# Batches three and four of an attention and mixer kernel: a head pair's scores in one piece of TensorE work, with two PSUM banks lent by the first channel product, its weighted sums in one piece, and hand-set places for both

## The chip, the cores and the metric

One core of a Trainium2 chip runs the whole program in one launch. The metric is device time in microseconds (us), the median of several executions. TensorE (PE) multiplies matrices into PSUM, which has eight banks of 512 fp32 columns on 128 partitions; VectorE (DVE) and ScalarE (ACT) read PSUM; GpSimd (POOL) works on SBUF alone; SyncE (SP) issues nearly all DMAs, in order. Each engine runs its own queue in order and waits on semaphores for the others.

## The reference

Four batches, 8 heads, 768 positions, head dimension 64. Attention over a local window plus block summaries, then a mixer over tokens and one over channels:

```python
mask_l = np.abs(pos[:, None] - pos[None, :]) < 16
k_sum = k.reshape(B, H, nb, 32, D).max(axis=3); v_sum = v.reshape(B, H, nb, 32, D).mean(axis=3)
scores_l = np.where(mask_l, scale * q @ k.T, -1e9)
scores_s = scale * q @ k_sum.T + np.log(32)
a = softmax(concatenate([scores_l, scores_s]));  attn = a @ concatenate([v, v_sum])
x = attn, heads side by side                           # (4, 768, 512)
h = np.maximum(x.T @ w_tok1, 0) @ w_tok2;  u = x + h.T  # tokens: 768 -> 256 -> 768
out = u + np.maximum(u @ w_ch1, 0) @ w_ch2             # channels: 512 -> 1536 -> 512
```

## The kernel before, in words

The program is written as a list of pieces of work (`add`, L91), each with an engine, an estimated duration, what it reads and writes and a rank. `Plan` (L77) lays the list out in time with those estimates: whenever an engine is free it takes the ready piece of lowest rank, then the oldest. The order that comes out is fixed for each engine before the kernel runs. On the chip an engine that meets a piece whose inputs are not there waits, with all that is queued behind it. Buffers and PSUM banks are rings with a tag: a ring of n gives its next user the buffer of the user n places before, once all of that user's work is done (`_link`, L114).

While the channel products of batch b run, the attention and the token mixer of batch b+1 are put between them. The loop over b (L1622) has 24 slots: twelve steps f with 512 of the 768 positions (half 0), then twelve with 256 (half 1). In a slot `ch1` (L926) adds the first channel product of the next step: 12 matmuls into one bank (`hp`, ring "mm", 2 banks), a relu on ACT (L947), its rounding rest on DVE (L952). `ch2` (L962) adds the second product of this step: 12 matmuls into the banks acc0 to acc3 in half 0, acc0 and acc1 in half 1. Both have rank `R_W`, below that of attention, so they fill PE whenever nothing else is ready.

PSUM: two banks have the tag "att", two "mm", four "acc". In half 0 attention has "att" alone (`BANKS[0]`, L263); in half 1 it also has acc2 and acc3.

Attention goes by pairs of heads, four pairs a batch. In the third and fourth batch (`FAR = 2`) a pair takes these steps (`att_step`, L685, in the order `LATER`, L672):

- `scores(p, g)` for each half g of the positions (L438): 24 PE instructions into two banks `sc`, one for each head; then six times `lowest` on DVE (L478: adds the mask, writes the negated scores to the SBUF tile `e`, and gives the row's extreme) and six times the exponential on ACT (L488). PSUM is free after the last `lowest`.
- `turn_blocks(p, g)` (L575): a transpose of `e` on DVE (L583), one DMA to DRAM (`away`, L587), four DMAs back (`eT`, L602).
- `weighted(p)` (L612): for each head 24 PE instructions into a bank `av` (L630), the reciprocals (L643, L647), a scaling out of PSUM on DVE (L650). Then `turn_x` (L711) sends the result to DRAM, and `load_v` fetches the next values.

The tiles `e`, `eT` and `xb` of `turn_x` share the ring "e" of three. `tok2` (L852) is the second token product for a pair and half: 6 PE instructions into a bank `up` (L874), an addition of the residual `xT` on DVE (L891), and a split into two parts (L901, L907). For half 1 it stands in slots 2 to 5 of the batch's own loop (`u1s`, L1632), with `fetch_x` (L733) one slot ahead, four DMAs to `xT`. The attention steps of the next batch are spread evenly over slots `a0` to `a1` (L1630, L1679). In the loop of b = 2, `weight_away` (L1102) writes one 512 KB block of weights to DRAM in each of slots 12 to 23. A Strassen-like scheme (`last_mix`, L1176) does the last batch's channel products after the loops.

Of the kernel before, what the change touches and what calls it, by code (L numbers as in the profile page):

```python
# [24 lines left out]
P = 128  # L25
# [177 lines left out]
def tile_attention_mixer(  # L203
# [234 lines left out]
    def scores(p, g, behind=()):  # L438

        kt, qt = k_t[p], q_t[p]  # L440
        tiles = []
        e = e_t[p, g] = sbuf([P, 2, HS], "e", f"e_{p}_{g}", 3)
        if p >= FAR * NP:

            add(
                "pool", 0.2,
                lambda: nc.gpsimd.memset(
                    e.t.rearrange("p j (t c) -> p (j t) c", c=P)[:, :, NC:], 0.0
                ),
                writes=[(e, "ends")], rank=R_LATER,  # L450
            )
        for j in range(2):
            n = 2 * p + j
            if g == 0:
                den_t[n] = sbuf([P, 2, TT], "den", f"den_{n}", 5)
            tiles.append(att_bank(f"sc_{n}_{g}"))

        def products():
            for i in range(TT // 2):
                for c in range(2):  # L460
                    t = 2 * (TT // 2 * g + i) + c
                    for j in range(2):
                        rows = slice(j * D, (j + 1) * D)
                        nc.tensor.matmul(  # L464
                            tiles[j].t[c * QT : (c + 1) * QT, i * NC : (i + 1) * NC],
                            lhsT=qt.t[rows, t * QT : (t + 1) * QT], rhs=kt.t[rows, t, :],
                            start=True, stop=True,
                        )
# [6 lines left out]
        def lowest(n, j, i):  # L475
# [3 lines left out]
                out=e.t[:, j, i * P : i * P + NC],  # L479
                in0=tiles[j].t[:, i * NC : (i + 1) * NC],  # L480
# [4 lines left out]
        def power(n, j, i):  # L485
            T = TT // 2 * g + i
            ei = e.t[:, j, i * P : i * P + NC]
# [8 lines left out]
        for j, i in parts:  # L496
                n = 2 * p + j
                den, T = den_t[n], TT // 2 * g + i
# [1266 lines left out]
```

## Time and profile before

| | us |
|---|---|
| median of 3 runs (549.94 to 551.34) | 551.19 |
| the profiled execution | 551.51 |
| its span, first to last instruction | 549.4 |

The profile gives, for each engine, every instruction with its start and duration, what ended the idle time ahead of it, and a chain of waits followed back from the last instruction. The duration of a matmul in the timeline includes a modelled end that overlaps the next one, so the cost of a piece of PE work is read from its start to the start of the next piece. PEld is the weight load that belongs to each matmul and overlaps others. The loop of b = 1, which carries the third batch's attention, runs from 191 to 323 us; the loop of b = 2, with the fourth's, from 323 to 457.

### The profile page before, as it was taken

The page shows a single profiled execution, that of the slowest core. Times are in us where ns is not written, and L with a number is a line of the kernel's source. Part 1 is how long each engine was busy: PE and PEld are TensorE (multiplying, and loading weights), DVE is VectorE, ACT ScalarE, POOL GpSimd, SP SyncE. Part 2 cuts the span into 40 slices and gives each one's busy share as a digit, 9 for nine tenths or more (in the row PEclk, how much of TensorE's full clock was granted, in tenths as well). Part 3 has the DMA queues.
Part 4 walks back from the last instruction along what each step waited for, and adds up shares of the span by engine and source line. Part 5 has one row for each costly group of instructions (what it writes and reads, how often), then busy time and mean ns, then how long its engine had stood idle before and what let it go on. Part 6 is the DMA issues. An engine that isn't in the chain of part 4 may idle for free.

```text
span 549.4 us, 12914 instructions
## 1 busy us (share of the span) xinstructions
PE 538.9 (98%) x4649; PEld 477.7 (87%) x4649; DVE 341.4 (62%) x954; ACT 268.9 (49%) x771; POOL 268.8 (49%) x348
## 2 busy tenths in 40 slices
PE   7999999999999999999999999999999999999997
PEld 4789888878999978788899988878799999999997
DVE  4996778667556654565653536544443584787886
ACT  4897888755574242223342334322334443566652
POOL 2656688713036110398996220069979602445111
PEclk9999999999999999999999999999999999999999
DMA  8963798664658357869796427668787654543521
GB/s 323 397 202 116 220 269 241 205 189 143 213 150 249 64 143 169 240 195 274 189 279 165 68 56 187 162 177 235 193 247 241 184 225 144 181 135 118 189 98 57
DMA packets 148127, 103.46 MB, mean 188 GB/s; under 512 B 101216, under 2 KB 126048, under 8 KB 148064
## 3 DMA queue, kind: packets, MB, share of 16 engines
q1 hardware_dynamic: 147920, 102.55, 63.2%
q8 instruction: 36, 0.59, 0.4%
q14 instruction: 27, 0.22, 0.1%
q10 hardware_dynamic: 144, 0.10, 0.1%
HBM read 70.96 MB, written 29.88 MB: 184 GB/s over the span
## 4 chain that ended last, share of the span: by engine, by line
PE 88%; DMA 6%; SPq 1%; issue 1%; ACT 1%; POOL 1%; DVE 0%; DVEq 0%; POOLq 0%; ACTq 0%
PE acc L978 26%; PE hp L935 25%; PE up L874 6%; PE t1q L833 5%; PE av L630 4%; PE pb L1213 3%; PE qb L1213 3%; PE sc L464 3%; PE qc L1213 2%; PE pa L1213 2%; PE pc L1213 2%; PE qa L1213 2%; PE t1p L785 2%; DMA w<-in_w_tok 2%; DMA vw<-in_vw 2%; DMA q<-in_q 1%
## 5 line engine op out<-in xcount | busy, mean ns | idle before, releaser
L978 PE MATMUL acc<-h,w 128*128 128x512 f32 (+1 forms) x864 | 162.2, 337 | 0.0
L935 PE MATMUL hp<-u,w 128*128 128x512 f32 (+1 forms) x864 | 161.1, 336 | 0.0
L935 PEld LDWEIGHTS hp<-u,w 128*128 128x128 f32 x864 | 132.9, 188 | 18.0 <-issue 1.3
L978 PEld LDWEIGHTS acc<-h,w 128*128 128x128 f32 x864 | 131.8, 188 | 19.0 <-ACT h L947 1.7
L947 ACT ACTIVATE h<-hp 128x512 fp32r<-128x512 f32 (+1 forms) x72 | 35.3, 490 | 121.2 <-PE hp L935 118.8
L488 ACT ACTIVATE e<-e,den 128x120 f32<-128x120 f32 x192 | 69.9, 385 | 49.0 <-DVE den L478 43.1
L952 DVE SCALAR_TENSOR_TENSOR h<-hp,h 128x512 fp32r<-128x512 f32 (+1 forms) x72 | 39.9, 554 | 70.6 <-ACT h L947 70.1
L1055 POOL TENSOR_TENSOR s<-s,w 128x256 f32<-128x256 f32 x84 | 62.2, 745 | 5.2
L478 DVE CUSTOM_DVE_ANT_0 e<-sc,mask_sb 128x120 f32<-128x120 f32 x192 | 41.5, 277 | 11.1 <-PE sc L464 7.9
L1017 POOL TENSOR_TENSOR ot<-ot,u 128x512 f32<-128x512 f32 (+1 forms) x24 | 23.7, 1013 | 41.4 <-issue 14.0
L1584 POOL TENSOR_TENSOR w<-wb,w 128x256 fp32r<-128x256 f32 x48 | 34.6, 742 | 11.5 <-ACT w L1578 11.2
L819 POOL TENSOR_TENSOR xs<-x,xs 128x512 fp32r<-128x512 f32 x18 | 23.5, 1308 | 32.5 <-ACT xs L814 32.5
L874 PE MATMUL up<-wt,t 128*128 128x512 f32 (+2 forms) x192 | 38.0, 340 | 0.6 <-DVE den L478 0.6
L874 PEld LDWEIGHTS up<-wt,t 128*128 128x128 f32 x192 | 30.7, 189 | 3.8 <-issue 1.0
L420 DVE TENSOR_REDUCE vs<-vb 96x8 f32<-96x256 f32 (+1 forms) x40 | 18.2, 460 | 18.0 <-DMA vb<-in_vb 18.0
L833 PE MATMUL t1q<-xs,ws 128*128 128x256 f32 x216 | 28.5, 283 | 0.0
L464 PEld LDWEIGHTS sc<-k,q 64*64 64x64 f32 x768 | 20.2, 132 | 9.4 <-issue 6.3
L464 PE MATMUL sc<-k,q 64*64 64x120 f32 x768 | 27.2, 271 | 0.9 <-DVE k L1057 0.9
L630 PEld LDWEIGHTS av<-v,eT 120*64 120x64 f32 x768 | 23.9, 138 | 4.6 <-issue 3.5
L351 DVE TENSOR_REDUCE ks<-k 128x24 f32<-128x768 f32 x16 | 15.1, 947 | 20.0 <-DMA k<-in_kw 20.0
L630 PE MATMUL av<-v,eT 120*64 120x64 f32 (+1 forms) x768 | 26.3, 224 | 0.9 <-DMA eT<-away 0.9
L833 PEld LDWEIGHTS t1q<-xs,ws 128*128 128x128 f32 x216 | 26.9, 190 | 0.2
(131 smaller groups left out, 849.6 us busy)
## 6 DMA issues: line engine op xcount, KB each, us to landing
w<-in_w_ch SPq DMA_DIRECT2D x48, 256.0 KB, 3.9
k<-in_kw SPq DMA_DIRECT2D x16, 720.0 KB, 6.7
v<-in_vw SPq DMA_DIRECT2D x24, 288.0 KB, 3.7
q<-in_q SPq DMA_DIRECT2D x16, 384.0 KB
away<-e SPq DMA_DIRECT2D x16, 384.0 KB, 3.1
eT<-away SPq DMA_DIRECT2D x64, 96.0 KB, 2.9
sums<-s SPq DMA_DIRECT2D x24, 256.0 KB, 2.9
w2d<-w SPq DMA_DIRECT2D x12, 512.0 KB, 4.5
```

Of the source, the lines that this page charges most:

```text
L464: nc.tensor.matmul(tiles[j].t[c * QT : (c + 1) * QT, i * NC : (i + 1) * NC], lhsT=qt.t[rows, t * QT : (t + 1) * QT], rhs=kt.t[rows, t, :], ...
L478: nc.vector.tensor_tensor_reduce(out=e.t[:, j, i * P : i * P + NC], in0=tiles[j].t[:, i * NC : (i + 1) * NC], in1=mask_sb[:, mv, :], op0=A ...
L488: nc.scalar.activation(ei, ei, AF.Exp, bias=den_t[n].t[:, 1, T : T + 1], scale=-1.0, accum_out=den_t[n].t[:, 0, T : T + 1] if p >= NP else ...
L630: nc.tensor.matmul(pv[cs, T], lhsT=eT(T % (TT // 2), c), rhs=v.t[:NC, 2 * T + c], start=True, stop=True,)
L833: nc.tensor.matmul(pt.t[:, 2 * P * k : 2 * P * (k + 1)], lhsT=ws[:, wp, T, ks], rhs=xs[:, xp, T], start=(c == 0 and k == 0 and T == 0 and ...
L874: nc.tensor.matmul(pt.t[:, :nt], lhsT=t1.t[:, part, ks], rhs=wt2[w].t[:, k, h0 : h0 + nt], start=(far and k == 0 and i == 0), stop=(k == D ...
L935: nc.tensor.matmul(pt.t[:, :nt], lhsT=w1_t[f].t[:, w, c], rhs=us[c].t[:, part], start=(i == 0), stop=(i == len(ops) - 1),)
L947: lambda: nc.scalar.activation(h.t[:, 0], pt.t[:, :nt], AF.Relu),
L952: lambda: nc.vector.scalar_tensor_tensor(out=h.t[:, 1], in0=pt.t[:, :nt], scalar=0.0, in1=h.t[:, 0].bitcast(F32), op0=ALU.max, op1=ALU.sub ...
L978: nc.tensor.matmul(slot.t[:, c0 : c0 + nt], lhsT=w2_t[f].t[:, w, o * P : (o + 1) * P], rhs=h.t[:, part], start=(f == 0 and w == 0 and part ...
L1055: nc.gpsimd.tensor_tensor(out=out_, in0=left, in1=right, op=op)
L1213: nc.tensor.matmul(bank_.t[:, cs], lhsT=w(i), rhs=x(j)[:, cs], start=first and n == 0, stop=True, skip_group_check=True,)
```

## The change

For the third and fourth batch `scores` takes both halves of a pair at once: 48 PE instructions as one piece into four banks. In half 0 the banks of the first half are taken from the ring "mm", those of the second from "att"; in half 1 all four from the attention ring. `weighted` hands PE both heads' products as one piece. The even spread gives way to a table, `PLACES`: scores of a batch's pairs (with their two `turn_blocks`) in slots -1 (the last slot of the loop before), 2, 6 and 11, weighted sums in slots 0, 6, 11, 17 (third batch) and 2, 6, 11, 14 (fourth). In half 1 `tok2` takes "mm" banks for some pairs (`NEAR`) and stands in slots 2, 2, 3, 3 and 0, 1, 2, 2. Five of the twelve `weight_away` go to the end of the loop of b = 1, the rest to slots 17 to 23 of b = 2. Instructions on data, their shapes and their number stay the same.

```diff
-    def scores(p, g, behind=()):
+    def scores(p, gs, behind=()):
...
+        tiles, wide = {}, len(gs) > 1
+        for g in gs:
+            e = e_t[p, g] = sbuf([P, 2, HS], "e", f"e_{p}_{g}", 3)
...
+            for j in range(2):
+                n = 2 * p + j
+                if g == 0:
+                    den_t[n] = sbuf([P, 2, TT], "den", f"den_{n}", 5)
+                near = wide and g == 0 and state["phase"] == 0
+                tiles[g, j] = (mm_bank if near else att_bank)(f"sc_{n}_{g}")
 
         def products():
-            for i in range(TT // 2):
...
+            for g in gs:
+                for i in range(TT // 2):
+                    for c in range(2):
+                        t = 2 * (TT // 2 * g + i) + c
+                        for j in range(2):
...
         add(
-            "pe", 0.95, products, reads=[(qt, 0), (kt, 0), (kt, 1)],
-            writes=[(t, 0) for t in tiles], rank=R_H, behind=behind,
+            "pe", 1.55 if wide else 0.95, products, reads=[(qt, 0), (kt, 0), (kt, 1)],
+            writes=[(t, 0) for t in tiles.values()], rank=R_H, behind=behind,
         )
...
-        for j, i in parts:
+        for g in gs:
+            for j, i in parts:
...
@@ weighted
-            add(
-                "pe", 0.8, products, reads=eT_t[n, 0][1] + eT_t[n, 1][1] + [(v, 0), (v, 1)],
-                writes=[(pt, 0)], rank=R_H,
-            )
+            reads = eT_t[n, 0][1] + eT_t[n, 1][1] + [(v, 0), (v, 1)]
+            whole += [(products, reads, pt)]
+            if b < FAR:
+                add("pe", 0.8, products, reads=reads, writes=[(pt, 0)], rank=R_H)
+            elif j:
+                runs, reads, banks = zip(*whole)
+                add(
+                    "pe", 1.6, lambda: [run() for run in runs], reads=sum(reads, []),
+                    writes=[(pt, 0) for pt in banks], rank=R_H,
+                )
...
@@ att_step
-        LATER += [("e", hp, 0), ("e", hp, 1)] + [("s", hp + 1, 0)] * more
-        LATER += [("a", hp, 0)] + [("s", hp + 1, 1)] * more
+    PAIR = [("s", None), ("e", 0), ("e", 1), ("a", 0)]
...
-        kind, hp, g = (LATER if b >= FAR else ORDER if b else FIRST)[s]
+        if b >= FAR:
+            hp, (kind, g) = s // 4, PAIR[s % 4]
+        else:
+            kind, hp, g = (ORDER if b else FIRST)[s]
...
-            scores(p, g, behind)
+            scores(p, (0, 1) if g is None else (g,), behind)
...
-            if g == 0 and p not in (NP - 1, 2 * NP - 1):
+            if g != 1 and p not in (NP - 1, 2 * NP - 1):
                 key_blocks(p + 1)
-            if b and g == 1 and p + 2 < B * NP and (b > 1 or hp < NP - 2):
+            if b and g != 0 and p + 2 < B * NP and (b > 1 or hp < NP - 2):
                 load_k(p + 2)
                 load_q(p + 2)
@@ tok2
+    NEAR = (0, 1, 2), (0, 2)
...
-        pt = tok_bank(f"up_{b}_{half}_{p}")
+        name = f"up_{b}_{half}_{p}"
+        pt = mm_bank(name) if b and half and p in NEAR[b > 1] else tok_bank(name)
@@ the loop
+    PLACES = {2: {}, 3: {}}
+    for b, ss, aa in ((2, (-1, 2, 6, 11), (0, 6, 11, 17)), (3, (-1, 2, 6, 11), (2, 6, 11, 14))):
+        for hp in range(NP):
+            PLACES[b].setdefault(ss[hp], []).extend(range(4 * hp, 4 * hp + 3))
+            PLACES[b].setdefault(aa[hp], []).append(4 * hp + 3)
...
-            a0, a1 = 0, 29
             t1s = (18, 20)
-            u1s = (2, 3, 4, 5)
+            u1s = ((2, 2, 3, 3), (0, 1, 2, 2))[b - 1]
...
-                if b >= XFAR and u1s[p] == slot + 1:
+                if b >= XFAR and slot == max(u1s[p] - 1, 0):
                     fetch_x(b, 1, p)
...
+            else:
+                steps = PLACES[b + 1].get(slot, ())
...
-            if b == B - 2 and slot >= NF:
+            if b == B - 3 and slot >= 2 * NF - 5:
+                weight_away(slot - 2 * NF + 5)
+            if b == B - 2 and slot >= NF + 5:
                 weight_away(slot - NF)
...
+            if slot == 2 * NF - 1 and b + 2 < B:
+                for s in PLACES[b + 2].get(-1, ()):
+                    att_step(b + 2, s, here)
             ch2(b, half, f)
```

## Rows read from the trace of the kernel before

**Rows 1.** The page's first two parts: busy time of each engine, its share of the span and its instructions; then the clock granted to TensorE in 40 equal slices, in tenths of full speed (9 is 90% or more).

```profile
PE 538.9 (98%) x4649; PEld 477.7 (87%) x4649; DVE 341.4 (62%) x954; ACT 268.9 (49%) x771; POOL 268.8 (49%) x348
PEclk9999999999999999999999999999999999999999
```

**Rows 2.** The timeline of PE at the start of the loop of b = 1: start us, duration us, line, output and inputs, shape, count of instructions, and in brackets idle time ahead and what ended it.

```profile
194.53 3.01 PE L935 MATMUL hp<-u,w 128*128 128x512 f32 x12
197.47 0.85 PE L464 MATMUL sc<-k,q 64*64 64x120 f32 x24
...
201.84 0.95 PE L874 MATMUL up<-wt,t 128*128 128x256 f32 x6 [0.58 <-DVE den L478]
202.62 2.89 PE L935 MATMUL hp<-u,w 128*128 128x512 f32 x12
205.44 0.85 PE L464 MATMUL sc<-k,q 64*64 64x120 f32 x24
206.22 3.02 PE L978 MATMUL acc<-h,w 128*128 128x512 f32 x12
209.08 2.88 PE L935 MATMUL hp<-u,w 128*128 128x512 f32 x12
211.80 0.88 PE L874 MATMUL up<-wt,t 128*128 128x256 f32 x6
```

**Rows 3.** The timeline of PE in the first batch, where both halves of a pair's scores stand side by side, and the weight loads (PEld) of that piece and of a single one.

```profile
12.90 1.46 PE L464 MATMUL sc<-k,q 64*64 64x120 f32 x48 [0.85 <-DVE k L1057]
14.29 0.55 PE L560 MATMUL et<-identf,e 128*120 128x128 f32 x3
...
12.87 1.26 PEld L464 LDWEIGHTS sc<-k,q 64*64 64x64 f32 x48 [1.07 <-PE et L560]
...
205.44 0.62 PEld L464 LDWEIGHTS sc<-k,q 64*64 64x64 f32 x24 [0.35 <-issue]
206.22 0.76 PEld L978 LDWEIGHTS acc<-h,w 128*128 128x128 f32 x4 [0.16 <-ACT h L947]
```

**Rows 4.** The timeline of PE at weighted sums of the third and fourth batch: 48 instructions are both heads.

```profile
242.57 1.62 PE L630 MATMUL av<-v,eT 120*64 120x64 f32 x48
244.12 2.11 PE L935 MATMUL hp<-u,w 128*128 128x512 f32 x8
...
346.31 1.62 PE L630 MATMUL av<-v,eT 120*64 120x64 f32 x48
...
367.87 0.57 PE L630 MATMUL av<-v,eT 120*64 120x64 f32 x12
369.36 1.27 PE L630 MATMUL av<-v,eT 120*64 120x64 f32 x36 [0.92 <-DMA eT<-away]
```

**Rows 5.** The chain of waits in order of time: start us, us, what; the weighted sums of the third batch's first pair.

```profile
218.14 1.74 PE av L630 x48
```

**Rows 6.** The timeline of ACT, DVE and PE: the evacuation of the `hp` product that began at 202.62; score chunks on DVE (the first and the last of six that ran without a wait, then two that waited, one with the end of its six); and the channel piece that followed the scores of that last one.

```profile
205.61 0.60 ACT L947 ACTIVATE h<-hp 128x512 fp32r<-128x512 f32 x1 [1.42 <-PE hp L935]
207.92 0.65 DVE L952 SCALAR_TENSOR_TENSOR h<-hp,h 128x512 fp32r<-128x512 f32 x1
...
200.60 0.27 DVE L478 CUSTOM_DVE_ANT_0 e<-sc,mask_sb 128x120 f32<-128x120 f32 x1
201.61 0.28 DVE L478 CUSTOM_DVE_ANT_0 e<-sc,mask_sb 128x120 f32<-128x120 f32 x1
...
210.29 0.28 DVE L478 CUSTOM_DVE_ANT_0 e<-sc,mask_sb 128x120 f32<-128x120 f32 x1 [0.69 <-DMA away<-e]
...
364.79 0.28 DVE L478 CUSTOM_DVE_ANT_0 e<-sc,mask_sb 128x120 f32<-128x120 f32 x1 [1.76 <-DMA away<-e]
366.01 0.09 DVE L478 DVE_READ_ACCUMULATOR2_ANT den<- 128x1 f32 x1
...
359.48 3.02 PE L978 MATMUL acc<-h,w 128*128 128x512 f32 x12
```

**Rows 7.** The timeline of SP's DMA queue: fetches of `eT`, the load of `k` ahead of a write `away` that landed late (issued at 357.88), and the fetch that waited for it.

```profile
236.31 2.67 SPq L602 DMA_DIRECT2D eT<-away  x4
...
338.59 5.47 SPq L602 DMA_DIRECT2D eT<-away  x8
...
355.10 0.59 SPq L291 DMA_DIRECT2D k<-in_kw  x1
...
364.67 2.67 SPq L602 DMA_DIRECT2D eT<-away  x4
```

**Rows 8.** DMA issues, from the page's last part: count, KB each, median us to landing.

```profile
eT<-away SPq DMA_DIRECT2D x64, 96.0 KB, 2.9
```

**Rows 9.** Channel pieces of half 1 with nothing between them, and two that have other pieces nearby (timeline of PE); then the stretches that `weight_away` enters and leaves: length, busy us of PE, PEld, DVE, ACT and POOL with counts, granted clock, DMA share, GB/s.

```profile
315.57 1.58 PE L935 MATMUL hp<-u,w 128*128 128x256 f32 x12
316.98 1.58 PE L978 MATMUL acc<-h,w 128*128 128x256 f32 x12
...
290.29 1.52 PE L935 MATMUL hp<-u,w 128*128 128x256 f32 x12
291.65 1.52 PE L978 MATMUL acc<-h,w 128*128 128x256 f32 x12
...
302.00:322.00 20.00, 20.00 (x162) 19.52 (x161) 9.00 (x15) 6.06 (x13) 3.35 (x5) 1.00 0.30 49
402.00:438.00 36.00, 36.00 (x317) 35.21 (x316) 14.99 (x29) 12.75 (x28) 28.66 (x28) 1.00 0.75 219
```

More of the change, by code (lines that the diff above doesn't have):

```diff
@@ new lines, in scores @@
+        tiles, wide = {}, len(gs) > 1
+        for g in gs:
+            e = e_t[p, g] = sbuf([P, 2, HS], "e", f"e_{p}_{g}", 3)
+            if p >= FAR * NP:
+                add(
+                    "pool", 0.2,
+                    lambda e=e: nc.gpsimd.memset(
+                        e.t.rearrange("p j (t c) -> p (j t) c", c=P)[:, :, NC:], 0.0
+                    ),
+                    writes=[(e, "ends")], rank=R_LATER,
+                )
[5 more added lines that the diff above has]
+                tiles[g, j] = (mm_bank if near else att_bank)(f"sc_{n}_{g}")
@@ new lines, in products @@
+        def products():
+            for g in gs:
[3 more added lines that the diff above has]
+                        for j in range(2):
+                            rows = slice(j * D, (j + 1) * D)
+                            nc.tensor.matmul(
+                                tiles[g, j].t[c * QT : (c + 1) * QT, i * NC : (i + 1) * NC],
+                                lhsT=qt.t[rows, t * QT : (t + 1) * QT], rhs=kt.t[rows, t, :],
+                                start=True, stop=True,
+                            )
@@ L478, in lowest @@
             nc.vector.tensor_tensor_reduce(
-                out=e.t[:, j, i * P : i * P + NC],
-                in0=tiles[j].t[:, i * NC : (i + 1) * NC],
+                out=e_t[p, g].t[:, j, i * P : i * P + NC],
+                in0=tiles[g, j].t[:, i * NC : (i + 1) * NC],
                 in1=mask_sb[:, mv, :], op0=ALU.add, op1=ALU.min,
@@ L617, in weighted @@
         x_t[b, hp] = x2, hp % 2
+        whole, rest = [], []
         for j in range(2):
@@ L654, in scaled @@
                 )
-            add(
-                "pe", 0.8, products, reads=eT_t[n, 0][1] + eT_t[n, 1][1] + [(v, 0), (v, 1)],
-                writes=[(pt, 0)], rank=R_H,
-            )
+            reads = eT_t[n, 0][1] + eT_t[n, 1][1] + [(v, 0), (v, 1)]
[4 more added lines that the diff above has]
+                runs, reads, banks = zip(*whole)
+                add(
+                    "pe", 1.6, lambda: [run() for run in runs], reads=sum(reads, []),
+                    writes=[(pt, 0) for pt in banks], rank=R_H,
+                )
+            rest += [(inverse, scaled, pt, den, rec, j)]
+        for inverse, scaled, pt, den, rec, j in rest:
+            n = 2 * p + j
             add(
@@ L1678, in tile_attention_mixer @@
                         vb_step(b + 2, 2 * (slot - m0) + c)
-            want = -(-(start[slot + 1] - a0) * STEPS // (a1 - a0))
-            steps = range(done, max(done, min(STEPS, want)))
-            done = steps.stop
+            if b + 1 < FAR:
+                want = -(-(start[slot + 1] - a0) * STEPS // (a1 - a0))
+                steps = range(done, max(done, min(STEPS, want)))
+                done = steps.stop
+            else:
+                steps = PLACES[b + 1].get(slot, ())
             for s in steps:
```

42 lines of the change are left out of this document (10 added, 32 removed).

## The prediction, as it was put on record

> **What bounds the kernel now.** First the page's busy shares and its 40 slices: PE is busy 98% of the span, at the upper of its two clock levels (2.4 GHz) from end to end, with no other engine over 62% [rows 1]. The reader should see that the clock has nothing to give and that a change pays only in what PE does or waits for. The change adds and removes no instruction, so I look for two things: what PE loses where a small piece of work stands between large ones, and where it stands idle. I take both from PE's timeline in the two loops that the change touches, 191 to 457 us, since PE is booked solid there: the idle time that is shown in it is 0.58 us ahead of an `up` [rows 2] and 0.92 us inside one pair of weighted sums [rows 4].
>
> **The price of a small piece.** From start to start, a 512-column channel piece with like pieces on both sides takes 211.80 - 209.08 = 2.72 us. With scores ahead of it, it takes 209.08 - 206.22 = 2.86; with scores ahead and behind, 197.47 - 194.53 = 2.94. So going into scores costs 0.08 and coming out 0.14. The 24 score instructions take 206.22 - 205.44 = 0.78 [rows 2]. A half's scores thus cost PE 0.78 + 0.22 = 1.00 us, a pair's 2.00.
>
> **Part 1, scores in one piece.** In the first batch both halves happen to stand side by side: 48 instructions in 14.29 - 12.90 = 1.39 us, not 2 x 0.78 = 1.56. The weight loads show why: 24 take 0.62 us and then nothing for 0.16 until the next piece's load; 48 take 1.26 [rows 3]. The wait at the end is paid once. A pair in one piece costs 1.39 + 0.22 = 1.61, so it saves 2.00 - 1.61 = 0.39; eight pairs, 3.1 us. The lower bound leaves the inside of the piece as it is, at 0.78 a half: 0.22 x 8 = 1.8 us. I take 3.1, since that row is the very piece, with the same shapes and at the same clock. All this lies on PE, which sets the end, so nothing hides it or eats it but new waits.
>
> The Trainium skill, "TensorEngine Tiling (Array Packing)", section Key Properties, says that changing the tiling mode drains TensorE. The trace agrees as to the large pieces (0.22 us a visit), and by that rule alone the sum would be the lower bound, 1.8.
>
> DVE and ACT keep their 12 `lowest` and 12 exponentials a pair. DVE's run at 201.61 - 200.60 = 1.01 us for five, 0.20 each [rows 6], off PE's path as long as no bank is awaited. The `memset` on POOL for a pair's two `e` tiles, POOL's sums behind it, and the loads of `k` and `q` on SP move with the scores. POOL is busy 49% of the span, and the weight sums that it does there are used only after the loops, so I put that at nothing; if that cover went, a late split of `u` would first be felt at the channel product of half 1, tens of us later.
>
> **Part 2, weighted sums in one piece.** Here I expect nothing. Both heads already stand side by side: 48 instructions in 244.12 - 242.57 = 1.55 us, and of the pairs shown only one is split [rows 4]. What changes is the wait. A pair's 48 now wait for both heads' `eT` and both banks ahead of the first one. In the split pair PE did 12 of its 48 and stood 0.92 for the rest; as one piece it would have stood ahead of all 48, some 0.5 us longer. Behind it on PE are channel products, in order, so such a wait is a loss to the end. The fetches land about 2.9 us after their issue [rows 8]: the last of four at about 238.3 lands at 241.2, 1.4 ahead of the `av` at 242.57; the last of eight at about 343.4 lands at 346.3, just when `av` starts at 346.31 [rows 4, 7]. The `av` at 218.14 takes 1.74 in place of 1.55, 0.19 lost [rows 5]. The order on PE is thus laid right on the landings, and the estimate is off by up to one us either way. I expect the same of the new order: eight places, about 0.92 + 0.19 = 1.1 us lost in sum, as now. Bounds: nothing (a gain of 1.1) to 0.92 at six of them, 5.5 (a loss of 4.4).
>
> **Part 3, the idle 0.58 us.** The `up` at 201.84 waited for the last `lowest` on its "att" bank [rows 2]. It now takes an "mm" bank, and the scores ahead of it stand in the loop before. I count 0.58 as gained; what is next there is the second channel product, whose input is ready once one more channel piece has run.
>
> **Part 4, "mm" banks lent.** In half 0 the ring runs hp, score bank, score bank, hp. So the scores wait until the `hp` before them is evacuated, and the `hp` after them until the first half's six `lowest` are done. First wait: the `hp` from 202.62 ended near 205.4, its relu began at 205.61, but its DVE part came only at 207.92 and ended 208.57, 3.1 us after the product [rows 6]. One channel piece of 2.72 to 2.86 covers it but for 0.2 to 0.4. Second wait: the six `lowest` need 1.2 us; after the first half's products the second half's (some 0.64) and a channel piece (2.86) run, so about 2 us are to spare. Queued behind the waiting scores or `hp` is all of PE. There are six such places (slots 2, 6, 11 of two loops). `up` in "mm" is covered in the same way, one DVE addition a bank. Bounds: below nothing I see no gain beyond part 3, since each bank is taken from the product that fills PE; above, 0.4 at each, 2.4. I take 0.5 in all.
>
> **Part 5, the moved steps.** Between slots 12 and 17 fewer small pieces are left. Channel pieces of half 1 that follow each other alone take 316.98 - 315.57 = 1.41 us; where token products stand nearby I read 291.65 - 290.29 = 1.36 [rows 9]. About four more at 1.41: 0.2 us lost. The five `weight_away` go into a stretch where DMA is at 0.30 of its share and leave one at 0.75 [rows 9]. PE shows no wait for DMA in either, so I put it at nothing; without that cover it would be an `xT` fetch late by one 512 KB write, some 2 us, behind which the next loop's first `hp` waits.
>
> **Sum.** -3.1 - 0.58 + 0 (weighted sums wait as now) + 0.5 + 0.2 = -3.0 us. The profiled execution took 551.51 us, 2.1 more than its span and 0.3 more than the median; 551.51 - 3.0 = 548.5, on the median's scale 551.19 - 3.0 = 548.2.
>
> **The rivals.**
> *The waits go too.* Pairs get four to six slots of up to 5.4 us each from scores to weighted sums, and the `k` load that delayed the `away` at 357.88 (issued at 355.10, the fetch only at 364.67) [rows 7] would be issued some 5 us ahead of the writes, the time of the 12 chunks and transposes. Then 1.1 more is gained and part 4 is nothing: -3.1 - 0.58 - 1.1 + 0.2 = -4.6, 546.6. Against it: the list takes `av` as early as its estimate allows, whatever the slots.
> *Weighted sums stand for their DMAs.* Eight fetches now follow two writes in one burst (5.5 us of issues [rows 7]), and all of it gates one piece. At 0.4 to 0.9 us for each of eight pairs, 3.2 to 7.2 in place of 1.1: 550.3 to 554.3, likeliest 551.0, the gain eaten.
> *The lent banks stop the channel products: slower.* Place: the `hp` after each of the six scores. Price: score banks are now often held long, since `lowest` writes to the ring "e" and waits for the write `away`: for the scores that ended at 206.22 the first began at 210.29; for those that ended at 359.48 the first began at 364.79 after a wait, and the last ended at 366.10, 6.6 us after its scores [rows 2, 6]. The cover from the first half's products is some 3.5 us, so beyond that lag every us stops PE; at 6.6 it is 3.1, six times 18.6 less 3.0 gained: 566.8; at two of six, 554.4. Against it: in the new order a pair's scores wait for the "att" banks of the weighted sums before them, and those free just the `eT` tiles that the new `e` needs. So `e` should be free when the scores run. The Trainium skill's same page, section PSUM Bottleneck, holds that tiling speeds up TensorE but not the evacuation of PSUM, which is this rival's rule; the 0.20 us a chunk speaks against it here.
> *It doesn't do what it says.* The scores are one piece but the price of a visit turns out not to be saved inside it: the lower bound, -1.8 - 0.58 + 0.7 = -1.7, 549.5. It is the forecast's upper edge.
>
> **How the numbers follow.** Forecast with its lower-bound case 0.47, waits gone 0.20, weighted sums standing 0.22, banks stopping PE 0.11. The range reaches from a little below the second, with part 5 at nothing and all bounds good (545.7), to 551.8 in the third; beyond lie the fourth and the third's worse half, about 0.18. A difference of 0.3%, 1.65 us, is about what a measurement tells from none: faster means below 549.5. That takes 0.45 of the forecast and all of the second, with 0.02 of the third: 0.67. Within 0.3%: 0.02 of the forecast and 0.17 of the third and 0.01 of the fourth: 0.20. Slower: 0.03 of the third and 0.10 of the fourth: 0.13.
>
> **What would show it.** Right: score runs of 48, eight in the two loops, 1.39 to 1.45 us from start to start; no idle ahead of `up`; `hp` after scores without idle. Wrong: 48 taking 1.56 (part 1's lower bound); idle ahead of `av` from the DMA `eT` at many pairs (part 2); idle at L935 or L464 ended by DVE `den` or `h` (part 4); idle at `up` in the new slots.

## The result, and the profile after

| | before | after |
|---|---|---|
| median (11 runs each), us | 551.19 | 554.05 |
| lowest to highest of them | 549.94 to 553.02 | 551.72 to 560.24 |
| the profiled execution; its span | 551.51; 549.4 | 553.85; 552.1 |

The ratio of after to before is 1.0052, 95% interval 1.0029 to 1.0075: slower by half a per cent. A gain of 3.0 us was forecast and a loss of 2.9 came; the time lies above the range. One slow run of after (560.24 us, mean clock 0.992) and one of G1 below (880.28 us, 0.557) are left out of their ratios.

The page of after, busy times and the clock in 40 slices, beside [rows 1]:

```profile
PE 537.2 (97%) x4649; PEld 479.3 (87%) x4649; DVE 341.5 (62%) x954; ACT 267.5 (48%) x771; POOL 268.0 (49%) x348
PEclk9999999999999999899999999999999999999999
```

PE does its work in 1.7 us less busy time, and the span is 2.7 longer. One slice of the clock, 221 to 235 us, shows an 8. So the loss is idle time and clock. The change moved the lines of the kernel: in the lines of after, `hp` is at L955, its relu at L967 and its rounding rest `h` at L972, the second product at L998, `sc` at L467, `av` at L636, `up` at L894 and the addition of `xT` at L911. What PE waited for between 183 and 500 us (us in all, times, longest):

```profile
PE acc L998 <- DVE h L972: 2.8, 2, 2.1
PE av L636 <- DVE xT L911: 1.7, 1, 1.7
PE av L636 <- DMA eT<-away: 1.0, 1, 1.0
PE up L894 <- DVE den L481: 0.2, 1, 0.2
```

Only the third line is a wait that the forecast had priced; the fourth is of the kind that part 3 counted as gone (0.58 before). Nothing stands at L955 or L467: neither the lent banks nor the merged scores stopped PE where the third rival looked. The timeline of PE in after (start, duration, work; idle ahead in brackets), beside [rows 2, 4]:

```profile
214.75 1.46 PE L467 MATMUL sc<-k,q 64*64 64x120 f32 x48
216.13 3.02 PE L998 MATMUL acc<-h,w 128*128 128x512 f32 x12
...
226.27 0.61 PE L998 MATMUL acc<-h,w 128*128 128x512 f32 x2
228.98 3.64 PE L998 MATMUL acc<-h,w 128*128 128x512 f32 x10 [2.09 <-DVE h L972]
232.42 3.47 PE L955 MATMUL hp<-u,w 128*128 128x512 f32 x12
235.73 2.88 PE L998 MATMUL acc<-h,w 128*128 128x512 f32 x12
...
345.11 0.92 PE L636 MATMUL av<-v,eT 120*64 120x64 f32 x24
347.75 0.92 PE L636 MATMUL av<-v,eT 120*64 120x64 f32 x24 [1.72 <-DVE xT L911]
```

The 48 score instructions take 216.13 - 214.75 = 1.38 us, as forecast (all eight such pieces take 1.39), and behind each of the eight stands a second product. The second product at 226.27 gets through 2 of its 12 matmuls and stands 2.09 us for the rounding rest of `h`, which is DVE's. DVE's timeline and, as the last line, the chain of waits (start, us, what) say why:

```profile
226.51 0.95 DVE L351 TENSOR_REDUCE ks<-k 128x24 f32<-128x768 f32 x1 [1.38 <-DMA k<-in_kw]
227.38 0.97 DVE L588 STREAM_TRANSPOSE e<-e 128x768 f32<-128x768 f32 x1
228.27 0.65 DVE L972 SCALAR_TENSOR_TENSOR h<-hp,h 128x512 fp32r<-128x512 f32 x1
```

```profile
220.21 6.28 DMA k<-in_kw
```

The load of the next `k`, issued at 220.21, landed at 226.49. In DVE's fixed order the reduction of that `k` stands ahead of a transpose and of `h`, so DVE stood 1.38 us and both came late. The load was not a slow one: the page of before gives 6.7 us as the median of `k`, while the list reckons with 737 / 250 + 2.1 = 5.0 when no transfer is ahead of it (L303, L79 and L161 of the kernel after). In windows (length, busy us of PE, PEld, DVE, ACT, POOL, clock, DMA share, GB/s) the stand is followed by a lower clock:

```profile
225.00:229.00 4.00, 1.91 (x10) 1.25 (x8) 2.62 (x5) 0.60 (x1) 3.77 (x6) 1.00 0.55 215
229.00:232.40 3.40, 3.40 (x10) 2.68 (x11) 2.40 (x5) 0.00 (x0) 3.17 (x5) 0.68 0.87 201
232.40:236.00 3.60, 3.60 (x15) 2.91 (x14) 0.41 (x1) 0.07 (x1) 0.20 (x1) 0.83 0.82 143
```

The clock was at 1.00 up to 229 us and fell after PE had stood; 0.68 and 0.83 are means of the two levels, 1.2 and 2.4 GHz. The lower level cost 3.40 x 0.32 + 3.60 x 0.17 = 1.7 us. The same from the rows above: the product after the stand takes 235.73 - 232.42 = 3.31 us where 2.72 was the price, and ten matmuls take 3.44 where 10/12 of 2.72 is 2.27, 1.76 in sum.

The second stand, at 347.75, is a PSUM bank. DVE and SP's queue:

```profile
344.51 0.42 DVE L911 TENSOR_TENSOR xT<-up,xT 128x256 f32<-128x256 f32 x1 [4.09 <-DMA xT<-xaway]
347.27 0.42 DVE L911 TENSOR_TENSOR xT<-up,xT 128x256 f32<-128x256 f32 x1 [2.33 <-DMA xT<-xaway]
```

```profile
336.00 5.54 SPq L607 DMA_DIRECT2D eT<-away  x8
341.58 3.94 SPq L607 DMA_DIRECT2D xT<-xaway  x6
```

`up` holds its bank until `xT` is added. In the new slots the fetches of `xT` are issued behind eight `eT` fetches, which take SP 5.54 us, so DVE stood 4.09 and 2.33 us for `xT`, and the second head's weighted sums waited for that bank.

DVE stood for loads in the old kernel too. Its waits for three of them, 186 to 456 us, in before and then in after (us in all, times, longest):

```profile
DVE vs L420 <- DMA vb<-in_vb: 14.5, 12, 3.6
DVE ks L351 <- DMA k<-in_kw: 11.9, 5, 4.2
DVE xT L891 <- DMA xT<-xaway: 1.3, 1, 1.3
...
DVE vs L420 <- DMA vb<-in_vb: 18.9, 8, 5.0
DVE xT L911 <- DMA xT<-xaway: 11.6, 4, 4.1
DVE ks L351 <- DMA k<-in_kw: 2.2, 2, 1.4
```

Those for `k` even fell, from 11.9 us to 2.2. In before 27.7 us of such stands went with 1.5 us of PE's idle time, and none of that was a wait for `h` or `xT`; so what counts is what is queued behind a stand, and not its length alone. Those for `xT` are new.

**The account.** For each kernel I take the stretch from the start of the last 512-column `up` ahead of the third batch's loop (near 184 us) to the end of the span. Idle is the sum of PE's idle times there; clock is (1 - granted clock) times length, over windows of 10 us; the rest is net work.

| kernel | stretch | idle | clock | net work |
|---|---|---|---|---|
| before | 365.4 | 1.5 | 0 | 363.9 |
| after | 368.7 | 5.6 | 1.7 | 361.3 |
| difference | +3.2 | +4.1 | +1.7 | -2.6 |
| forecast | -3.0 | -0.1 | 0 | -2.9 |

The clock's part is not in every run: in the ten runs of after in the ratio the mean clock is 0.999 or more in six, with spans of 549.1 to 552.0 (mean 550.7), and 0.996 to 0.997 in four (mean 553.0). Idle and net work without the clock make 4.1 - 2.6 = 1.5 us, and the six lie 550.7 - 549.4 = 1.3 above the profiled execution of before. That the idle time belongs to the order and not to one execution I take from this agreement; only the profiled one shows it.

### The profile page after: what moved, and what is told of

It reads as the page before. It is cut to its first block, busy times and chain, and to the rows that moved or that the text cites. A ratio compares the mean times of both kernels' runs of the same rounds, so it can differ in the third digit from the quotient of the medians.

```text
span 552.1 us, 12921 instructions
## 1 busy us (share of the span) xinstructions
PE 537.2 (97%) x4649; PEld 479.3 (87%) x4649; DVE 341.5 (62%) x954; ACT 267.5 (48%) x771; POOL 268.0 (49%) x348
## 4 chain that ended last, share of the span: by engine, by line
PE 76%; DMA 7%; DVE 6%; SPq 5%; POOL 3%; issue 1%; ACT 1%; DVEq 0%; ACTq 0%; POOLq 0%
PE acc L998 22%; PE hp L955 20%; PE up L894 5%; PE t1q L850 5%; SPq L607 4%; PE pb L1233 3%; PE qb L1233 3%; PE av L636 3%; DMA k<-in_kw 3%; PE sc L467 2%; PE qc L1233 2%; PE pa L1233 2%; PE pc L1233 2%; PE qa L1233 2%; POOL s L1075 2%; PE t1p L802 2%
## 5 line engine op out<-in xcount | busy, mean ns | idle before, releaser
L998 PE MATMUL acc<-h,w 128*128 128x512 f32 (+1 forms) x864 | 163.4, 338 | 2.8 <-DVE h L972 2.8
L955 PE MATMUL hp<-u,w 128*128 128x512 f32 (+1 forms) x864 | 160.1, 336 | 0.0
L998 PEld LDWEIGHTS acc<-h,w 128*128 128x128 f32 x864 | 133.0, 189 | 22.2 <-DVE h L972 3.4
L955 PEld LDWEIGHTS hp<-u,w 128*128 128x128 f32 x864 | 133.7, 189 | 17.9 <-issue 0.8
L967 ACT ACTIVATE h<-hp 128x512 fp32r<-128x512 f32 (+1 forms) x72 | 35.3, 491 | 132.9 <-PE hp L955 124.2
L972 DVE SCALAR_TENSOR_TENSOR h<-hp,h 128x512 fp32r<-128x512 f32 (+1 forms) x72 | 39.9, 555 | 73.8 <-ACT h L967 73.4
L481 DVE CUSTOM_DVE_ANT_0 e<-sc,mask_sb 128x120 f32<-128x120 f32 x192 | 41.2, 277 | 11.9 <-PE sc L467 11.7
L1604 POOL TENSOR_TENSOR w<-wb,w 128x256 fp32r<-128x256 f32 x48 | 34.6, 742 | 11.9 <-ACT w L1598 11.7
L894 PE MATMUL up<-wt,t 128*128 128x512 f32 (+2 forms) x192 | 37.9, 341 | 0.3 <-DVE den L481 0.2
L894 PEld LDWEIGHTS up<-wt,t 128*128 128x128 f32 x192 | 30.6, 189 | 3.5 <-DVE h L972 0.5
L636 PEld LDWEIGHTS av<-v,eT 120*64 120x64 f32 x768 | 23.9, 138 | 6.5 <-issue 3.6
L636 PE MATMUL av<-v,eT 120*64 120x64 f32 (+1 forms) x768 | 26.3, 224 | 2.7 <-DVE xT L911 1.7
L491 ACT ACTIVATION_READ_ACCUMULATOR e<-e,den 128x1 f32 x144 | 27.2, 189 | 0.0
L467 PE MATMUL sc<-k,q 64*64 64x120 f32 x768 | 25.1, 269 | 1.1 <-DVE k L1077 1.1
L836 POOL TENSOR_TENSOR ws<-wt,ws 128x512 fp32r<-128x512 f32 x18 | 23.8, 1322 | 4.0 <-ACT ws L831 4.0
```

What stands on the lines that cost most here:

```text
L467: nc.tensor.matmul(tiles[g, j].t[c * QT : (c + 1) * QT, i * NC : (i + 1) * NC], lhsT=qt.t[rows, t * QT : (t + 1) * QT], rhs=kt.t[rows, t, ...
L481: nc.vector.tensor_tensor_reduce(out=e_t[p, g].t[:, j, i * P : i * P + NC], in0=tiles[g, j].t[:, i * NC : (i + 1) * NC], in1=mask_sb[:, mv ...
L491: nc.scalar.activation(ei, ei, AF.Exp, bias=den_t[n].t[:, 1, T : T + 1], scale=-1.0, accum_out=den_t[n].t[:, 0, T : T + 1] if p >= NP else ...
L636: nc.tensor.matmul(pv[cs, T], lhsT=eT(T % (TT // 2), c), rhs=v.t[:NC, 2 * T + c], start=True, stop=True,)
L836: lambda slot=slot, src=src: nc.gpsimd.tensor_tensor(out=slot.t[:, 1], in0=src(), in1=slot.t[:, 0].bitcast(F32), op=ALU.subtract),
L894: nc.tensor.matmul(pt.t[:, :nt], lhsT=t1.t[:, part, ks], rhs=wt2[w].t[:, k, h0 : h0 + nt], start=(far and k == 0 and i == 0), stop=(k == D ...
```

## The experiments

Theory A: the merge saves what it should, and the moved places give it back through loads that have not landed when an in-order engine meets them. Rival B: lending "mm" banks makes the channel products wait for score chunks wherever these stand. Rival C: the moved `weight_away` crowd the DMAs. Each ratio is to runs of before timed beside it, with its 95% interval; idle, clock and net work are those of the one profiled execution. An edit of an estimate lays the order of every engine anew, so such a run prices an order and not a single wait.

**E1: the reduction of `k` behind the score chunks.**

```diff
-    def key_blocks(p):
+    def key_blocks(p, behind=()):
...
-                key_blocks(p + 1)
+                key_blocks(p + 1, behind if g is None else ())
```

(The DVE reduction gets `behind=behind`.)

> The changed kernel, but the key maxima of the next pair (the reduction on DVE that waits for the load of k) may start only after the gate of the slot in which the scores before them stand, so that DVE no longer meets them before the load has landed. Theory (waits by the order on DVE, then the clock): the 2.09 us that the second channel product stood near 227 us for h on DVE and the 1.76 us of lower clock behind it go, 3.5 to 3.9 us less than the changed kernel, near 550.2 us, with the granted clock at 1.00 there. Rival (the lent banks, or the new order on PE as such, cost the time): the wait stays or moves to another hp or acc piece, 553 to 555 us.

Measured: 555.00 us, ratio 1.0075 (1.005 to 1.0101), the rival's time; idle 7.0, clock 3.4 in the profiled execution, the slowest of the eight (558.09). The stand for `h` near 229 is gone and another has come, in PE's timeline and in a window (columns as above):

```profile
236.60 0.57 PE L636 MATMUL av<-v,eT 120*64 120x64 f32 x12 [0.77 <-DMA eT<-away]
239.83 2.19 PE L636 MATMUL av<-v,eT 120*64 120x64 f32 x36 [2.66 <-DMA eT<-away]
```

```profile
240.00:244.00 4.00, 4.00 (x41) 3.50 (x41) 2.81 (x5) 0.00 (x0) 1.98 (x5) 0.50 0.56 155
```

The write `away` took 8.91 us from issue to landing there (3.1 is the median of before), and `eT` came late. One wait taken out alone bought nothing: the next late transfer takes its place, and the clock is at its lower level behind it, as it was in after.

**E2: `tok2` in its old slots and bank.**

```diff
-        pt = mm_bank(name) if b and half and p in NEAR[b > 1] else tok_bank(name)
+        pt = tok_bank(name)
...
-            u1s = ((2, 2, 3, 3), (0, 1, 2, 2))[b - 1]
+            u1s = (2, 3, 4, 5)
```

> The changed kernel with the second token product of half 1 as it was: slots 2 to 5, banks of the attention ring, no mm bank. Theory (waits by order): the 1.72 us that weighted sums stood at 346 us for a bank held by up, whose residual came late from DRAM, is bound to the early slots; with the old slots it goes or shrinks, 1 to 2 us less than the changed kernel, 552 to 553 us; the wait of 2.09 us near 227 for DVE stays unless the order on DVE shifts by chance. Rival (the mm banks lent to up stop the channel products): 3 us or more less, and no idle at all ahead of channel pieces.

Measured: 550.28, ratio 0.9992 (0.9977 to 1.0007); idle 3.6, clock 0, net 361.0. So the new slots and banks of `tok2` cost, with all that they shift, 1.0052 - 0.9992 = 0.6%, 3.3 us. The time is the rival's, but its sign, no idle time ahead of channel pieces, is not there. The 1.72 for `xT` is gone, and the stand for `h` with it but for 0.4; what is left besides is three waits for `eT` (1.9 in all), and one for a lent bank:

```profile
219.99 2.99 PE L955 MATMUL hp<-u,w 128*128 128x512 f32 x12 [1.31 <-DVE den L481]
```

```profile
218.41 0.42 DVE L420 TENSOR_REDUCE vs<-vb 96x8 f32<-96x256 f32 x1 [0.67 <-DMA vb<-in_vb]
218.75 0.27 DVE L481 CUSTOM_DVE_ANT_0 e<-sc,mask_sb 128x120 f32<-128x120 f32 x1
```

Rival B's wait exists, then. Here DVE stood 0.67 for a load of `vb` with the chunks behind it. The other 1.31 - 0.67 = 0.64 is the time of the chunks: `hp` stands directly behind the scores on PE, with no second product between them as in after.

**E3: the even spread of before, with `tok2` and `weight_away` as before.** The merged pieces alone.

```diff
-                steps = PLACES[b + 1].get(slot, ())
+                want = -(-(start[slot + 1]) * 4 * NP // (26 if b == B - 2 else 29))
+                steps = range(done, max(done, min(4 * NP, want)))
+                done = steps.stop
```

(Slot -1 is dropped; the edits of E2 and E4 are in it.)

> The changed kernel with only its first part: scores and weighted sums in one piece, mm banks lent to scores; the attention steps evenly spread over the slots as before, the second token products and the weight writes as before. Theory (one piece saves 0.39 us for each of eight pairs, the waits come from places and order): 48 score instructions in 1.39 us each; without new waits 548 to 549 us, and each us of PE idle beyond the 1.5 of the kernel before adds to that. Rival (lending the banks is what costs): idle of PE ahead of L955 or L467 after the scores of half 0, six times 0.4 us or more, 553 us or above.

Measured: 562.89, ratio 1.0211 (1.0183 to 1.0239); idle 12.1, clock 1.7. Five stands for lent banks make 5.6 us:

```profile
PE hp L955 <- DVE den L481: 5.6, 5, 2.3
PE av L636 <- DMA eT<-away: 2.9, 3, 1.9
```

The other 3.6 are waits for `h`. So merged pieces need places of their own; the table is no ornament. It is rival B's price (554.4 to 566.8) in another order than the change's, and the places show the reason. In three of the eight a second product follows the scores, and `hp` does not stand; in five `hp` follows them directly, and it stands in all five, in three of them 0.68 to 0.69 us while DVE was ready and waited for the scores. PE and the first chunk on DVE at one of these:

```profile
387.11 1.46 PE L467 MATMUL sc<-k,q 64*64 64x120 f32 x48
389.25 5.68 PE L955 MATMUL hp<-u,w 128*128 128x512 f32 x24 [0.68 <-DVE den L481]
```

```profile
388.00 0.28 DVE L481 CUSTOM_DVE_ANT_0 e<-sc,mask_sb 128x120 f32<-128x120 f32 x1 [2.18 <-PE sc L467]
```

Six chunks at 0.20 take until 389.2, and nothing on PE covers them. At the longest stand, 2.28 us, DVE came late as well: it had waited 1.10 for `vb` at 274.72 and came to the chunks at 278.44 by way of two scalings, two steps of the output, a transpose and a second `vb`. It waited for no buffer of the ring "e" at any of the five.

**E4: `weight_away` in its old slots.**

```diff
-            if b == B - 3 and slot >= 2 * NF - 5:
-                weight_away(slot - 2 * NF + 5)
-            if b == B - 2 and slot >= NF + 5:
+            if b == B - 2 and slot >= NF:
```

> The changed kernel with all twelve weight writes in the loop of b = 2, slots 12 to 23, as before. Theory: they meet no wait of PE; within 0.5 us of the changed kernel (553.5 to 554.6), the waits near 227, 346 and 394 us stay. Rival (moving five writes ahead of the fourth batch delays its first fetches): the 1.72 us at 346 go, 552.3 us.

Measured: 559.47, ratio 1.0151 (1.0127 to 1.0176); idle 7.9, clock 1.7, net 362.3. That is outside what either side expected (553.5 to 554.6, or 552.3). Rival C falls: the move gains 1%, 5.4 us. The loops themselves do end earlier without it, the first product of the last mix starting at 456.7 in place of 459.9, but the last mix gives back more. PE's timeline there and the chain:

```profile
468.69 1.57 PE L1233 MATMUL pb<-t,s 128*128 128x384 f32 x6 [2.79 <-ACT s L1245]
```

```profile
465.24 2.90 DMA s<-sums
```

A load of `sums` issued at 465.24 gates the product that stands 2.79 us. The last mix takes 99.6 us in place of 92.2; the stand and the clock behind it are 4.5 of that, the rest is shorter waits and other work in its order, which I did not follow further.

**G1: one estimate.** SP's issue of a fetch of 32 rows is put at 0.66 us, not 0.4, since eight took 5.5 us [rows 7].

```diff
-                "sp", 0.4, lambda r=r: part(r), reads=[(away, 0)], ...
+                "sp", 0.66, lambda r=r: part(r), reads=[(away, 0)], ...
```

> The changed kernel laid out with one estimate corrected: a fetch of 32 rows takes SP's queue 0.66 us to issue (measured 0.66) in place of 0.43. Nothing else differs; the order that comes out does. Theory (the loss is waits, because the fixed order is laid on estimates that run ahead of the chip's DMAs): PE's idle in the loops falls from 5.6 us to 3 or less and no fall of the clock follows; 549 to 551.5 us. Rival (the new structure needs these waits whatever the estimates): idle stays at 5 us or more in sum, at other places, 553 to 556 us.

Measured: 550.96, ratio 1.0002 (0.9987 to 1.0017); idle 3.6, clock 0. It gives back 0.5%, 2.8 us, as the theory had it, though idle stays above its 3 us and DVE still stands for `k`, 1.58 us at 226.91.

**G2, G3, G4: landings later and transfers slower.** After 185 us the estimated rate is 200 KB/us in place of 250 and the landing 3.2 us in place of 2.1, with G1's edit; on the change, with E2's edit, and on the kernel before.

```diff
-  dma = max(dma, w.start) + w.kb / (self.RATE if now > 30 else self.FIRST)
-  w.end = dma + self.LAND
+  dma = max(dma, w.start) + w.kb / (200.0 if now > 185 else self.RATE if now > 30 else self.FIRST)
+  w.end = dma + (3.2 if now > 185 else self.LAND)
```

> As the run with the corrected issue time, and from 185 us on a transfer is taken to land 1.1 us later (3.2 us after its data in place of 2.1) at 200 in place of 250 KB per us. Theory: weighted sums are then placed behind their landings, no wait of PE for the DMA eT is left over 0.3 us, the key reduction on DVE comes after its load; 547.5 to 550 us. Rival: the waits go elsewhere (banks held longer, as hp for DVE den), 553 us or above.

> Second token products as in the kernel before (slots 2 to 5, no mm bank) with both corrected estimates. Theory: the 3.6 us of waits that were left with the old token products (1.31 for DVE den, 1.93 for eT, 0.35 for h) halve; 547.5 to 549.5 us. Rival: one visit less for each pair saves less than 0.3 us when all is counted, and the time stays at 550 to 551.

> The kernel before with both corrected estimates and nothing of the change: the control. Theory (estimates cost any order some waits): its 1.7 us of idle and short stalls in the loops shrink, 549.8 to 551 us. Rival (the order of before was right by its own estimates and later placing only delays): 551.5 us or above.

Measured: 576.82 (1.0475, 1.0445 to 1.0504), 576.40 (1.0455, 1.043 to 1.048) and 588.21 (1.0671, 1.0649 to 1.0692). All far slower, the old kernel most, with PE's two longest stands in G4:

```profile
PE pb L1213 <- ACT s L1225: 11.3, 1, 11.3
PE av L630 <- DMA eT<-away: 8.4, 1, 8.4
```

None of the three expectations came. My reading, which no run shows, is that with every transfer put later the plan's DMA line runs ever further behind the chip's, and work is queued that could have run. "The estimates are too good" is thus no cure by itself; which transfer is put later decides.

**H1: landings at 3.1 us, rate unchanged, with G1's edit.**

```diff
-                    w.end = dma + self.LAND
+                    w.end = dma + (3.1 if now > 185 else self.LAND)
```

> The changed kernel, SP's issue time at 0.66 us and from 185 us on landings 1.0 us later than estimated, the transfer rate left at 250 KB per us. The 576 us of the runs with the rate at 200 may come from that rate (an estimated backlog that never was) or from later landings as such. Theory: from the rate, so this one stays within 548.5 to 551.5 us and no weighted sums wait for eT over 0.3 us. Rival (any later estimate lets pieces pile up): 555 us or more.

Measured: 557.41, ratio 1.0117 (1.0099 to 1.0135); the rival's time, so the rate was not all that was wrong with G2. Its longest stand is again a lent bank behind `vb`, on PE and on DVE:

```profile
280.77 2.90 PE L955 MATMUL hp<-u,w 128*128 128x256 f32 x12 [4.77 <-DVE den L481]
```

```profile
279.20 0.42 DVE L420 TENSOR_REDUCE vs<-vb 96x8 f32<-96x256 f32 x1 [3.29 <-DMA vb<-in_vb]
279.54 0.27 DVE L481 CUSTOM_DVE_ANT_0 e<-sc,mask_sb 128x120 f32<-128x120 f32 x1
```

**H2, H3, H4: G1's edit with E2's, with E1's, and on the kernel before.** The edits are those shown above.

> Second token products as in the kernel before (slots 2 to 5, no mm bank) and SP's issue time at 0.66 us, landings as estimated. Theory (waits by the order are the whole loss; the two edits each cut them to about 3.5 us): 2 to 3.5 us of idle, 549 to 550.5 us. Rival (each order draws its waits anew, so that the two do not add): 550.5 to 553 us.

> The changed kernel with SP's issue time at 0.66 us and the key reductions held back by the gate of their slot. In the run with the issue time alone DVE met a reduction 1.58 us ahead of its load at 226.9, and a channel product stood 1.23 for the h behind it. Theory: that wait goes and nothing as long takes its place, 549 to 550.5 us. Rival (as when the keys alone were held back, a wait for eT takes its place): 551 us or more.

> The kernel before with SP's issue time at 0.66 us and nothing of the change: the control for the run of the changed kernel with that estimate, 550.96. Theory (scores in one piece save 2.5 to 3 us of work at equal waits): with waits as in the kernel before this stays at 550.5 to 552 us, and its work, loops less idle, at 363.5 to 364 us against 361 of the changed kernel. Rival (the estimate is the gain, the merge none): 548.5 us or less.

Measured: 549.62 (0.9986, 0.9965 to 1.0007), 550.93 (0.9995, 0.998 to 1.001) and 552.44 (1.002, 1.0007 to 1.0034). H2 came as its theory had it, H3 between theory and rival, H4 0.4 above its theory's range. The estimate alone brings the kernel before nothing, so what it gives the change is repair of the change's own order. In H2 the waits between 186 and 456 us still show DVE standing for `vb`:

```profile
DVE vs L420 <- DMA vb<-in_vb: 18.5, 10, 3.5
```

**I1 to I4: only `vb` (and `k`) later.** After 185 us a load of `vb` is put 2.0 us later, one of `k` 1.5, so that DVE meets their reductions further down its list. All have G1's edit; I1 and I4 have E2's too; I2 keeps the change's `tok2`; I3 is the kernel before; I4 leaves `k` alone.

```diff
-                    w.end = dma + self.LAND
+                    w.end = dma + self.LAND + (w.late if now > 185 else 0.0)
...
-        load(slot, lambda t: t[:VB], vb[b, :, rows], 12 * n)
+        load(slot, lambda t: t[:VB], vb[b, :, rows], 12 * n).late = 2.0
```

> As the run with the old second token products and SP's issue time (549.62 us), and from 185 us on the list takes the loads of vb to land 2.0 us later and those of k 1.5 us later than its estimate, these two alone. Theory (DVE meets a reduction ahead of its load, in order, and with scores in lent banks that now stops the channel product): the waits of hp for DVE den (1.03 and 0.26 us) and those for h go; 547.5 to 549.5 us. Rival (each new order draws its waits anew): 550 us or more, with waits of another kind in their place.

> The changed kernel with its own token products, SP's issue time, and the same two loads later. Theory: no wait of a channel product for DVE over 0.5 us; 548.5 to 550.5 us, under its 550.96 without the loads' correction. Rival: 551 us or more.

> The kernel before with SP's issue time and the same two loads later: control. Theory: score banks of its own cover DVE's standing, so nothing is to be had; 551 to 553 us. Rival (the estimate alone is the gain): below 550 us.

> As the first, with only the loads of vb later. Theory (the wait at 220 us has its cause in a vb reduction ahead of the scores on DVE): the 1.03 us go as well; 548 to 550 us. Rival (it is the key reduction or DVE's own work): the wait of hp for den at about 220 us stays at 1 us.

| | us | ratio to before | idle | clock | net work |
|---|---|---|---|---|---|
| I1 | 547.42 | 0.9946 (0.9928 to 0.9964) | 1.0 | 0 | 360.6 |
| I2 | 549.64 | 0.9983 (0.9967 to 1.0) | 3.1 | 0 | 360.7 |
| I3, before | 549.88 | 0.9997 (0.998 to 1.0014) | 0.2 | 0 | 364.2 |
| I4 | 547.24 | 0.9945 (0.993 to 0.9959) | 1.0 | 0 | 360.4 |

I4 beats both kernels. What DVE and PE wait for in it, 186 to 456 and 183 to 500 us (its lines are three further down):

```profile
DVE vs L423 <- DMA vb<-in_vb: 2.1, 2, 1.8
```

```profile
PE hp L958 <- DVE den L484: 0.8, 2, 0.6
PE pb L1236 <- DVE s L1080: 0.2, 1, 0.2
```

DVE's stand for `vb` falls from 18.5 us to 2.1, and PE's idle from H2's 2.4 to 1.0. `vb` alone does it: I1 and I4 agree. At the lent banks only 0.5 of these 1.4 us is found (1.3 to 0.8): the wait of 1.03 near 220 us that I1 and I4 were to take away is still 0.58, with `hp` directly behind the scores. The rest, waits for `eT` and for a bank of `up`, went with the new order. In I2 one `up` still stands 1.58 us and one `hp` 0.69.

On the kernel before the same edits do nothing against before itself (I3, 0.9997), though DVE's stands for `vb` fall to 0.7 there too. Its 549.88 lies just under the 550 that the rival was given; but the runs of before timed beside it have a median of 550.44. I1 and I3 have the same two estimates and differ by the merge with its places, those of `weight_away` among them: 549.88 - 547.42 = 2.5 us gained, which is what is left of 3.1.

## Why the prediction was wrong

**Part 1 was right in mechanism and size.** 48 instructions in 1.39 us were found at all eight places where 1.39 was forecast, and net work fell by 2.6 us, 2.9 having been forecast for parts 1 and 5 together. The three orders without merged scores have 363.9 to 364.4 (before, H4, I3); with them, nine have 360.4 to 361.8 (after, E1, E2, G1, H2, H3, I1, I2, I4) and E4 and E3 362.3 and 362.7, while in G2 to G4 and H1 idle and clock are too large to be taken off well. Rival 4, "it doesn't do what it says", is out for the change: its lower bound, 1.8 less 0.2, would have left 362.3. That bound was what the Trainium skill's rule would give by itself, that a change of tiling mode drains TensorE ("TensorEngine Tiling (Array Packing)", Key Properties); no run here measures the drain by itself.

**Parts 2 and 4 are the terms that were mis-sized.** The forecast had 1.1 us of waits as now and 0.5 for lent banks, 1.6 in all, and PE stood 5.6. Of that, 1.0 us is `eT`, the wait of part 2, and it came as forecast ("about 1.1 us lost in sum, as now"). Another 0.2 is an `up` that waits for an "att" bank, the kind that part 3 counted as gone (0.58). None is the wait of part 4 at `hp` or at the scores: the channel piece on which part 4 counts as cover stands behind all eight score pieces. The rest, 2.8 for `h` and 1.7 for `xT`, has no line in the prediction. Two steps failed:

- *"DVE's run ... off PE's path as long as no bank is awaited."* The chunks were counted, 0.20 each, and POOL's and SP's moved steps were named. The reduction of `k` on DVE, which the code adds right behind the scores, was not. It moved with them, ahead of `h`, and its load had not landed. The duration (0.95) is harmless; the 1.38 us of standing for a load, with a transpose and `h` queued behind it, is what reached PE. E1 shows it for this place, since the stand is gone when the reduction goes down the list; the time did not fall with it, since other waits came.
- *"`up` in "mm" is covered in the same way, one DVE addition a bank."* Only the lent banks were looked at, and of the addition only its time. It is short, but its other operand is a fetch that now stands behind eight others on SP, and an "att" bank that it held late stopped the weighted sums. The new slots of `tok2` had no price at all. E2 shows that of slots and banks together, 3.3 us; the two were not tried apart, so how much is the slots' and how much the banks' stays open.

The 5.5 us of issues for eight fetches was in the prediction, used for the weighted sums alone; G1 shows that the list reckoned with 3.2 (8 x 0.4), and that this error is worth 2.8 us in the change; on the kernel before, mending it gains nothing (H4).

**The clock had no term.** "The clock has nothing to give" was right and half of the matter: it could take. 1.7 us of the profiled execution are the lower level after one stand of 2.09 us.

**Part 5.** `weight_away` at nothing was wrong in the other direction: putting it back costs 5.4 us (E4), in the last mix, where the prediction had not looked.

**The rivals.** "Weighted sums stand for their DMAs" came nearest in time (550.3 to 554.3) by luck, and not by its mechanism: that made 1.0 of the 5.6 us. "The lent banks stop the channel products" didn't happen in the change and did in E3 (5.6 us), H1 (7.7, the longest 4.77) and E2 (1.31). Its reason was mistaken: no chunk in these three runs stood for a buffer of the ring "e". The argument against it, that the `e` buffers should be free, was right and guarded the wrong door. What failed was part 4's cover, a channel piece behind the scores: without it the chunks' own time costs 0.68 to 0.69 us with DVE ready (E3). On top of that, at the longest stands, DVE was held by a load of `vb` with the chunks queued behind it (0.67, 1.10 and 3.29 us of its time). The Trainium skill's rule for this rival, that tiling speeds TensorE but not the evacuation of PSUM ("TensorEngine Tiling (Array Packing)", PSUM Bottleneck), holds here in this sense: chunks still follow each other at 0.20 us, as in [rows 6], and set when a lent bank is free; but I4 loses only 0.8 us to that in all.

## What to carry to other kernels

When a piece on a saturated engine is made larger or moved, list every step that the code issues with it, on every engine, and for each ask what its queue stands for if the input is late: a reduction of 0.95 us that stood for its load cost PE 2.09 us and 1.7 of clock, more than nine merged visits saved. The old kernel had such stands too, 26.4 us for `vb` and `k`, and PE lost nothing to them; how much of that its own score banks did, and how much its order, was not tried. So after lending buffers, keep a piece between the borrower and the owner that covers the borrower's time (E3), move load-dependent work behind what frees them (I4), one kind of load at a time, and try the same edits on the old kernel to see whose gain it is. Removing the wait that the profile shows need not help (E1), and putting all estimates later can be far worse (G2 to G4).

## What the runs showed of the hardware

- A single stand of PE brought the clock down to its lower level. It fell behind stands of 2.09 (after), 2.28 (E3), 2.66 (E1), 2.79 (E4) and 4.77 us (H1); behind single stands of 1.86 us or less (1.86 in E3, 1.72 in after, 1.58 in I2, 1.31 in E2) no window shows it. In G2 and G3 it also fell behind shorter stands close together (0.94 and 0.84 us within 2.2 us in G3). In after, E3 and E4 it cost 1.7 us an execution, 0.6 to 0.8 of the stand; in E1 3.2 of the 3.4 fell behind the stand, in H1 2.5 of 3.4, the rest into it.
- SP's median for issuing a 96 KB fetch `eT` was 0.66 us in before and after (0.56 to 2.03; eight in 5.47 and 5.54), and the loads queued behind them start that much later.
- One transfer can land far from the median of its kind: a write `away` in 8.91 us (E1), where the median of before is 3.1.
